# Four PSUM banks for scores, one for up products, and a plan that counts changes of kind on TensorE

## The chip, the cores and the metric

The kernel runs on one core of one Trainium2 chip. The metric is the device time of one execution in microseconds; lower is better. Five engines matter here: TensorE (PE in the profile; PEld is its weight load), VectorE (DVE), ScalarE (ACT), GpSimd (POOL) and SyncE (SP), whose queue issues nearly all DMAs.

## The reference

Attention with a compressive memory over B=4 batches, H=8 heads, S=576 rows and D=64, then two feed-forward layers over the 2304 rows of width 512, with 2048 hidden columns:

```python
scores = causal(scale * q @ k.T)                 # B,H,S,S
local = softmax(scores) @ v
q_p = phi(q)                                     # elu(q) + 1
mem_out = (q_p @ M_prev) / (q_p . z_prev + 1e-6)
a = g * mem_out + (1 - g) * local                # g = sigmoid(beta), one per head
x = a as [2304, 512]
h = x @ w_in;   x = where(h > 0, h, 0.01 * h) @ w_out      # layer 1
h = x @ w_in2;  x = (h - tanh(h)) @ w_out2                 # layer 2
```

## The kernel before

Attention is cut into 32 units (`UNITS`): a kind, a batch and a pair of heads. Kind B has query rows 256 to 575 (tiles 2, 3 and 4 of 128 rows, the last of 64) and runs first, kind A rows 0 to 255 (tiles 0 and 1). A unit loads queries and keys (`qk`) and values (`v` or `va`); multiplies phi(q) by the memory matrix (`mem`, L567); makes the scores (`score`, L647 and L652; two heads side by side on 64 rows of the array each), one group for each of B's three tiles and one for both of A's; VectorE masks them and takes the maximum (`maxi`, L673), ScalarE takes the exponential (L693), the rows are scaled (L727 to L731), TensorE transposes them (`tr_e`, L767 and L779) and multiplies by the values (`pv`, L801), whose PSUM tile begins with the transposed memory part (L745). Four units of one kind and batch make a block of 256 rows; the last 64 rows of every batch make a ninth.

Layer 1 of the first three blocks (`NARROW`) runs beside attention, in eight steps of two weight columns tiles each: an up product of 24 matmuls (L910) into the PSUM tile `up`, ScalarE's leak (L965) out of it, a split into two parts, and 24 down matmuls (L988) into `dn0` and `dn1`, which collect over all eight steps. The weights come as 32 pieces of 512 KB (`w`), which `convert` turns from 64-bit into two 32-bit parts (L838 to L854). The rest of layer 1 and all of layer 2 follow in a fixed loop (L1163 up, L1200 down).

The order of the first part is made when the kernel is built, by `Schedule`: every piece of work has a cost for each engine that could take it, a priority (smallest first) and the tiles that it reads, writes and takes. `run` goes through time and gives each free engine the first piece in order of priority that is ready and whose tiles are free; that order is then each engine's program. `RINGS` says how many buffers a tile has (`s`, `o`, `up`, `dn0` and `dn1` are PSUM banks: 3 + 1 + 2 + 1 + 1 = 8). A unit's priority is its place in `UNITS` plus `OFFSET` of its part; weight pieces have `W1_FROM` (the first 4 x `CUT` the first number, the others the second); TensorE's part of layer 1 comes after attention. `SWITCH` is what TensorE's change from one kind of work (0 layer 1, 1 scores and values, 2 transposes) to another costs. `CALM` holds weight loads back while the DMA queues are that far behind, `AHEAD` bounds how many pieces are in flight, `BIAS` weighs engines against each other. The first `LEND` units put their scores into banks that layer 1 needs later: tiles 2 and 4 into `up`, tile 3 into `dn0` and `dn1`. Units marked in `UNITS` keep their exponentials in tiles of late weights (`LENT`), which can load only after that. `EARLY` weight pieces are loaded at the very start on ScalarE's queue.

Of the kernel before, what the change touches and what calls it, by code (L numbers as in the profile page):

```python
# [9 lines left out]
F32 = mybir.dt.float32  # L10
# [34 lines left out]
SWITCH = {(0, 1): 88.0, (2, 1): 88.0, (0, 2): 45.0}  # L45

CALM = 6000.0
# [50 lines left out]
class Schedule:  # L98
# [60 lines left out]

    def pace(self, t):  # L160
# [24 lines left out]
    def run(self):  # L185
        engines = ("pe", "act", "dve", "pool", "sp")
        free = {"pe": 2500.0, "act": 2200.0, "dve": 3200.0, "pool": 4000.0, "sp": 800.0}
        ready = {e: [] for e in engines}

# [9 lines left out]
        mode = 0  # L199
        port_free = 0.0  # L200
        events = sorted(set(free.values()))
        t = -1.0
        while todo:
# [4 lines left out]
            t = nxt  # L208
            again = True
            while again:  # L210
                again = False
                for e in engines:
                    if free[e] > t:
                        continue
                    for i, (_, _, at, o) in enumerate(ready[e]):
# [56 lines left out]
OFFSET = {"load": 0, "memory": 0.3, "scores": -1, "values": 0.6}  # L272
# [3 lines left out]
LEND = 6  # L276
# [3 lines left out]
UNITS = [(k, b, hp, hp % 2 if k == "A" or b < 1 else 0) for k in "BA" for b in range(4) for hp in range(4)]  # L280
# [3 lines left out]
EARLY = 2  # L284

AHEAD = 5

BIAS = {"act": 1.0, "dve": 1.5, "pool": 1.1}

W1_FROM, W1_STEP = (7.7, 15.7), 0.002  # L290
# [3 lines left out]
CUT = 2  # L294
# [3 lines left out]
def kernel(  # L298
# [40 lines left out]

    early_raw = [wts.tile([128, 1024], I32, name=f"w0_{f}") for f in range(EARLY)]  # L340
# [9 lines left out]
    ginv = const.tile([128, H], F32, name="ginv")  # L350
# [79 lines left out]
    up_p = p1.enter_context(tc.tile_pool(name="up", bufs=2, space=PSUM))  # L430
# [8 lines left out]
    s_p = pa.enter_context(tc.tile_pool(name="s", bufs=3, space=PSUM, side="right"))  # L439
# [33 lines left out]
    class Unit:  # L473
# [14 lines left out]
        def declare(self, pr, prev):  # L488
# [104 lines left out]
            order["p"] = op([("pe", nq * 195)], mem, reads=[ph, mz], alloc=[s, mo], after=in_order("p"))  # L593
# [12 lines left out]
            for tiles in ([[0, 1]] if kind == "A" else [[2], [3], [4]]):  # L606
                if not self.lend:
                    ss = [new("s"), new("s")]
                elif tiles == [3]:
                    ss = [new("dn0"), new("dn1")]  # L610
                else:
                    ss = [new("up"), new("up")]
                c0 = 0
                for t in tiles:
                    nn = min(S, (t + 1) * 128)
                    if kind == "A":
                        et[t - q0] = new(f"e{t if self.alt else t + 2}")
                    else:
                        et[t - q0] = new(f"{'h' if self.alt else 'e'}{t}")
                        if self.alt:  # L620
                            lent.setdefault(LENT[t - 2], []).append(et[t - q0])
                    made[t] = (ss, new("mx"), c0)
                    c0 += nn
                width = c0 if tiles != [4] else S

                def score(e, tiles=tiles, ss=ss):
                    for s in ss:
                        if s.tag == "s":
                            s.tile = s_p.tile([128, 512], F32, name="s")
                        else:  # L630
                            pool = up_p if s.tag == "up" else dn_p
                            s.tile = pool.tile([128, 2, 256], F32, name=s.tag).rearrange("p a b -> p (a b)")
                    for t in tiles:
# [6 lines left out]
                        _, mx, c0 = made[t]  # L640
# [15 lines left out]
                order["s"] = op([("pe", {384: 847, 512: 1060, 576: 1117}[width])], score, reads=[qk], mode=1,  # L656
# [357 lines left out]
    def load_beta(e):  # L1014
        nc.sync.dma_start(out=ginv, in_=beta.partition_broadcast(128))
# [306 lines left out]
```

## Time and profile before

| | us |
|---|---|
| median of 3 runs (lowest, highest) | 1019.71 (1017.88, 1019.96) |
| profiled execution | 1019.15 |
| its span, first to last instruction | 1017.4 |
| TensorE busy | 995.1 |
| VectorE, ScalarE, GpSimd busy | 702.8, 629.6, 196.9 |

The profile is of one execution. Spans and busy times are on the time axis of its first instruction. A line such as L647 is a line of the kernel before. Matmuls are pipelined: their starts are recorded, their ends modelled, so the start of the next one says more than the length. The granted TensorE clock is 0.998 of full speed over the span.

### The profile page before, as it was taken

Reading aid. Unit: us, or ns where it says so; the run is one execution under the profiler, and the core shown is the slowest. Engines: PE = TensorE matmul, PEld = TensorE weight load, DVE = VectorE, ACT = ScalarE, POOL = GpSimd, SP = SyncE. Lnnn points to the kernel's source line nnn. Section 1 sums busy time; section 2 is a strip of 40 time slices with the busy share of each in tenths; the row PEclk is TensorE's granted clock in tenths of the full one; section 3 lists DMA queues with packets and bytes.
Section 4 is the critical chain, followed back from the end, with each engine's and each line's share of the span. In section 5 each row is a group of like instructions: output and inputs, shape, how many; then the busy total and the mean of one; then the engine's idle time right before and its main releaser. Section 6 shows DMA issues by size and latency. Waiting matters only on the chain.

```text
span 1017.4 us, 16055 instructions
## 1 busy us (share of the span) xinstructions
PE 995.1 (98%) x5664; PEld 817.5 (80%) x5664; DVE 702.8 (69%) x1592; ACT 629.6 (62%) x1325; POOL 196.9 (19%) x174
## 2 busy tenths in 40 slices
PE   5899999999999999999999999999999999999998
PEld 3577877778888988888888888888888888888897
DVE  7999999555577366758650225877787787777775
ACT  6987787666598244334423436866676676676664
POOL 1100000000000022222224553222222222222221
PEclk9999999999999999999999999999999999999999
DMA  9564622212252156446534333100100100010010
GB/s 273 188 184 128 192 91 70 69 49 70 59 154 79 63 161 221 144 138 196 184 106 142 117 94 94 43 1 0 63 21 1 63 22 1 1 62 1 1 43 21
DMA packets 92993, 91.77 MB, mean 90 GB/s; under 512 B 45296, under 2 KB 72944, under 8 KB 92912
## 3 DMA queue, kind: packets, MB, share of 16 engines
q1 hardware_dynamic: 91696, 89.44, 28.5%
q10 hardware_dynamic: 1216, 1.31, 0.4%
q8 instruction: 44, 0.72, 0.3%
q14 instruction: 37, 0.30, 0.1%
HBM read 69.75 MB, written 20.97 MB: 89 GB/s over the span
## 4 chain that ended last, share of the span: by engine, by line
PE 91%; DVE 5%; DMA 2%; ACT 1%; issue 1%; SPq 0%; ACTq 0%
PE up L1163 32%; PE dn L1200 32%; PE up L910 6%; PE dn L988 6%; PE o L801 4%; PE s L779 4%; PE s L647 3%; DMA qk<-in_qkt_dram 2%; PE s L567 1%; PE o L745 1%; PE s L652 1%; DVE e L673 1%; DVE cv L849 1%; DVE w L673 1%; DVE e L729 0%
## 5 line engine op out<-in xcount | busy, mean ns | idle before, releaser
L1163 PE MATMUL up<-xs,w 128*128 128x512 f32 (+1 forms) x1536 | 346.1, 375 | 0.0
L1163 PEld LDWEIGHTS up<-xs,w 128*128 128x128 f32 x1536 | 275.8, 188 | 52.9
L468 POOL TENSOR_TENSOR gl<-gf,gh 128x512 fp32r<-128x512 f32 x119 | 154.9, 1301 | 591.7 <-ACT gh L1150 579.5
L1200 PE MATMUL dn<-w,gh 128*128 128x512 f32 x576 | 174.8, 389 | 0.0
L1140 DVE SCALAR_TENSOR_TENSOR gf<-u,w 128x512 f32<-128x512 f32 x72 | 83.8, 1165 | 67.7 <-ACT w L1137 67.6
L1200 PEld LDWEIGHTS dn<-w,gh 128*128 128x128 f32 x576 | 107.6, 188 | 22.0
L1200 PE MATMUL dn<-gh,w 128*128 128x512 f32 x384 | 118.3, 389 | 0.0
L1200 PE MATMUL dn<-w,gl 128*128 128x512 f32 x288 | 109.5, 389 | 0.0
L1117 ACT ACTIVATE gf<-up 128x512 f32<-128x512 f32 x48 | 28.6, 597 | 119.7 <-PE up L1163 116.4
L1131 ACT ACTIVATE u<-up 128x512 f32<-128x512 f32 x72 | 43.0, 598 | 91.8 <-PE up L1163 91.6
L693 ACT ACTIVATE e<-e,mx 128x256 f32<-128x256 f32 (+4 forms) x134 | 76.0, 569 | 21.8 <-DVE mx L673 13.6
L910 PE MATMUL up<-xs,w 128*128 128x256 f32 x576 | 86.8, 290 | 0.0
L1150 ACT ACTIVATE gh<-gf 128x512 fp32r<-128x512 f32 x120 | 74.6, 621 | 16.9 <-DVE gf L1143 16.8
L1200 PEld LDWEIGHTS dn<-gh,w 128*128 128x128 f32 x384 | 72.1, 188 | 15.0
L910 PEld LDWEIGHTS up<-xs,w 128*128 128x128 f32 x576 | 73.6, 189 | 4.7 <-issue 4.7
L1200 PE MATMUL dn<-gl,w 128*128 128x512 f32 x192 | 74.7, 389 | 0.0
L1200 PEld LDWEIGHTS dn<-w,gl 128*128 128x128 f32 x288 | 54.0, 188 | 11.3
L455 ACT ACTIVATE pt<-s 128x320 f32<-128x320 f32 (+4 forms) x132 | 52.7, 440 | 15.9 <-PE s L779 9.3
L673 DVE CUSTOM_DVE_ANT_0 e<-s,mask 128x128 f32<-128x128 f32 (+4 forms) x114 | 46.8, 455 | 22.3 <-PE s L647 19.3
L779 PE MATMUL s<-identr,e 128*128 128x128 f32 x404 | 56.9, 279 | 4.4 <-ACT e L727 1.8
L1143 DVE COPY_PREDICATED gf<-mk,up 128x512 f32<-128x512 int32 x72 | 53.7, 746 | 7.4
L988 PE MATMUL dn<-gh,w 128*128 128x256 f32 x384 | 54.7, 286 | 0.4 <-ACT gh L455 0.4
(130 smaller groups left out, 1506.2 us busy)
## 6 DMA issues: line engine op xcount, KB each, us to landing
w<-in_moe_w_out_dram SPq DMA_DIRECT2D x16, 512.0 KB, 5.5
w<-vs SPq DMA_DIRECT2D x32, 256.0 KB, 2.6
qk<-in_qkt_dram SPq DMA_DIRECT2D x16, 448.0 KB, 3.6
w<-in_moe_w_in_dram SPq DMA_DIRECT2D x14, 512.0 KB, 5.8
v<-in_v_dram SPq DMA_DIRECT2D x16, 320.0 KB, 3.1
x2i<-x2s SPq DMA_DIRECT2D x9, 512.0 KB, 4.1
qk<-in_qkt_dram SPq DMA_DIRECT2D x16, 256.0 KB, 2.8
u<-in_moe_w_in_dram SPq DMA_DIRECT2D x16, 256.0 KB, 2.9
```

The source lines that it names most:

```text
L455: nc.scalar.activation(out=out, in_=in_, func=AF.Copy)
L468: (nc.vector if e == "dve" else nc.gpsimd).tensor_tensor(out=out, in0=in_, in1=high, op=ALU.subtract)
L673: nc.vector.tensor_tensor_reduce(out=out, in0=in0, in1=in1, scale=-scale, scalar=mx.tile[:, 0:1] if t == 4 and j else BIG, op0=ALU.add, op ...
L693: nc.scalar.activation(out=x, in_=x, func=AF.Exp, scale=-1.0, bias=mx.tile[:, k:k + 1], accum_out=sm.tile[:, 2 * i + j:2 * i + j + 1])
L779: nc.tensor.transpose(ss[j].tile[:, a:a + 128], x, ident)
L910: nc.tensor.matmul(ps()[:, s, :], lhsT=w[:, wh * 512 + kt * 128:wh * 512 + (kt + 1) * 128], rhs=xs()[:, xh, kt, :], start=(kt == 0 and j = ...
L988: nc.tensor.matmul(dn[m // 2].tile[:, m % 2, :], lhsT=w[:, wh * 512 + m * 128:wh * 512 + (m + 1) * 128], rhs=gg.tile[:, s * 256:(s + 1) * ...
L1140: nc.vector.scalar_tensor_tensor(out=g, in0=u, scalar=lin, in1=w, op0=ALU.mult, op1=ALU.add)
L1143: nc.vector.copy_predicated(out=g, mask=mk.bitcast(I32), data=h)
L1150: nc.scalar.activation(out=gh, in_=g, func=AF.Copy)
L1163: nc.tensor.matmul(ps[:, s * n:(s + 1) * n], lhsT=w[:, wh * 512 + kt * 128:wh * 512 + (kt + 1) * 128], rhs=xs[:, xh, kt, 0:n], start=(kt = ...
L1200: nc.tensor.matmul(dn, lhsT=lhs, rhs=rhs, start=(fs[0] == 0 and s == 0 and j == 0), stop=(f == NF - 1 and j == 2))
```

## The change

Scores get four PSUM banks instead of three, up products one instead of two. The first units (eight instead of six) borrow only `dn0` and `dn1`, for tile 3; tiles 2 and 4 go to the score banks. `Schedule` knows five kinds of work on TensorE (0 layer 1, 1 scores, 2 transposes, 3 memory products, 4 values) and a cost for every change between two of them, and the costs of the pieces themselves are set anew. Behind a score group it looks for another score group first, behind values for scores or values (`STICK`). Otherwise (`HOLD`) a score group that isn't `paired` comes last: paired means that its banks aren't only score banks, or that all four score banks are free and a second score group is ready or will be. Queries and keys get three buffers; the memory matrix and kind A's values get one each. No weight piece is loaded early; beta's load moves from SP to the start of ScalarE's queue. The order of the units, which of them use lent tiles, the offsets, the due times of the weights, `CALM`, `AHEAD` and `BIAS` get other values.

```diff
-    "qk": 2, "xr": 1, "mz": 2, "v": 1, "va": 2, "ph": 1, "dnm": 2, "mo": 1, "mx": 6, "sm": 3,
-    "e0": 1, "e1": 1, "e2": 1, "e3": 1, "e4": 1, "h2": 1, "h3": 1, "h4": 1, "s": 3, "o": 1, "pt": 4, "x": 2, "xs": 1,
-    "g": 2, "gl": 2, "gh": 2, "up": 2, "dn0": 1, "dn1": 1, "cv": 3,
+    "qk": 3, "xr": 1, "mz": 1, "v": 1, "va": 1, "ph": 1, "dnm": 2, "mo": 1, "mx": 6, "sm": 3,
+    "e0": 1, "e1": 1, "e2": 1, "e3": 1, "e4": 1, "h2": 1, "h3": 1, "h4": 1, "s": 4, "o": 1, "pt": 4, "x": 2, "xs": 1,
+    "g": 2, "gl": 2, "gh": 2, "up": 1, "dn0": 1, "dn1": 1, "cv": 3,
...
-SWITCH = {(0, 1): 88.0, (2, 1): 88.0, (0, 2): 45.0}
-
-CALM = 6000.0
+SWITCH = {
+    (0, 1): 188.0, (0, 2): 2.0, (0, 3): 108.0, (0, 4): 188.0, (1, 0): 209.0, (1, 2): 154.0, (1, 3): 307.0,
+    (1, 4): 200.0, (2, 0): 7.0, (2, 1): 187.0, (2, 3): 109.0, (2, 4): 191.0, (3, 0): 136.0, (3, 1): 324.0,
+    (3, 2): 134.0, (3, 4): 323.0, (4, 0): 206.0, (4, 1): 204.0, (4, 2): 154.0, (4, 3): 309.0,
+}
+
+STICK = {1: (1,), 4: (1, 4)}
+
+HOLD = True
+
+CALM = 20000.0
...
+    def paired(self, o, t):
+
+        if any(h.tag not in ("s", "mx") and h.tag[0] not in "eh" for h in o.alloc):
+            return True
+        free = sum(h is None or not (h.left or h.free_at > t) for h in self.rings["s"])
+        return free >= 4 and (
+            any(x.mode == 1 and x.left == 1 for x in o.users) or any(x[3].mode == 1 and x[3] is not o for x in self.line))
+
...
-                    for i, (_, _, at, o) in enumerate(ready[e]):
+                    line = ready[e]
+                    if e == "pe" and mode in STICK:
+                        line = sorted(line, key=lambda x: x[3].mode not in STICK[mode])
+                    elif e == "pe" and HOLD:
+                        line = sorted(line, key=lambda x: x[3].mode == 1 and not self.paired(x[3], t))
+                    for i, (_, _, at, o) in enumerate(line):
...
-OFFSET = {"load": 0, "memory": 0.3, "scores": -1, "values": 0.6}
+OFFSET = {'load': -0.4, 'memory': -0.1, 'scores': -1.2, 'values': 0.3}
...
-LEND = 6
+LEND = 8
+
+SETS = {"A": (((0, 1),),), "B": (((2,),), ((3,),), ((4,),))}
...
-UNITS = [(k, b, hp, hp % 2 if k == "A" or b < 1 else 0) for k in "BA" for b in range(4) for hp in range(4)]
+UNITS = [
+    ("B", 0, 0, 0), ("B", 0, 1, 1), ("B", 0, 2, 0), ("B", 0, 3, 1), ("B", 1, 0, 0), ("B", 1, 1, 0),
+    ("B", 1, 2, 0), ("B", 1, 3, 1), ("B", 2, 0, 0), ("B", 2, 1, 1), ("B", 2, 2, 0), ("B", 2, 3, 1),
+    ("B", 3, 0, 0), ("B", 3, 1, 0), ("B", 3, 2, 0), ("B", 3, 3, 0), ("A", 0, 0, 0), ("A", 0, 1, 1),
+    ("A", 0, 2, 1), ("A", 0, 3, 0), ("A", 1, 0, 0), ("A", 1, 1, 1), ("A", 1, 3, 1), ("A", 1, 2, 0),
+    ("A", 2, 0, 0), ("A", 2, 1, 1), ("A", 2, 2, 0), ("A", 2, 3, 1), ("A", 3, 0, 0), ("A", 3, 1, 1),
+    ("A", 3, 2, 0), ("A", 3, 3, 1),
+]
...
-EARLY = 2
-
-AHEAD = 5
-
-BIAS = {"act": 1.0, "dve": 1.5, "pool": 1.1}
-
-W1_FROM, W1_STEP = (7.7, 15.7), 0.002
+EARLY = 0
+
+AHEAD = 4
+
+BIAS = {'act': 0.9, 'dve': 1.6, 'pool': 0.8}
+
+W1_FROM, W1_STEP = (9.5, 42.0), 0.05
...
-CUT = 2
+CUT = 7
...
+    ginv = const.tile([128, H], F32, name="ginv")
+    nc.scalar.dma_start(out=ginv, in_=beta.partition_broadcast(128))
...
-    ginv = const.tile([128, H], F32, name="ginv")
...
-    up_p = p1.enter_context(tc.tile_pool(name="up", bufs=2, space=PSUM))
+    up_p = p1.enter_context(tc.tile_pool(name="up", bufs=1, space=PSUM))
...
-    s_p = pa.enter_context(tc.tile_pool(name="s", bufs=3, space=PSUM, side="right"))
+    s_p = pa.enter_context(tc.tile_pool(name="s", bufs=4, space=PSUM, side="right"))
...
-            order["p"] = op([("pe", nq * 195)], mem, reads=[ph, mz], alloc=[s, mo], after=in_order("p"))
+            order["p"] = op([("pe", {2: 206, 3: 429}[nq])], mem, mode=3, reads=[ph, mz], alloc=[s, mo], after=in_order("p"))
...
-            for tiles in ([[0, 1]] if kind == "A" else [[2], [3], [4]]):
-                if not self.lend:
-                    ss = [new("s"), new("s")]
-                elif tiles == [3]:
-                    ss = [new("dn0"), new("dn1")]
-                else:
-                    ss = [new("up"), new("up")]
-                c0 = 0
-                for t in tiles:
-                    nn = min(S, (t + 1) * 128)
-                    if kind == "A":
-                        et[t - q0] = new(f"e{t if self.alt else t + 2}")
-                    else:
-                        et[t - q0] = new(f"{'h' if self.alt else 'e'}{t}")
-                        if self.alt:
-                            lent.setdefault(LENT[t - 2], []).append(et[t - q0])
-                    made[t] = (ss, new("mx"), c0)
-                    c0 += nn
-                width = c0 if tiles != [4] else S
-
-                def score(e, tiles=tiles, ss=ss):
-                    for s in ss:
+            for group in SETS[kind]:
+                banks, cost = [], 0
+                for tiles in group:
+                    tags = ("s", "s")
+                    if self.lend and tiles == (3,):
+                        tags = ("dn0", "dn1")
+                    ss = [new(x) for x in tags]
+                    banks += ss
+                    c0 = 0
+                    for t in tiles:
+                        if kind == "A":
+                            et[t - q0] = new(f"e{t if self.alt else t + 2}")
+                        else:
+                            et[t - q0] = new(f"{'h' if self.alt else 'e'}{t}")
+                            if self.alt:
+                                lent.setdefault(LENT[t - 2], []).append(et[t - q0])
+                        made[t] = (ss, new("mx"), c0)
+                        c0 += min(S, (t + 1) * 128)
+                    cost += {384: 656, 512: 859, 576: 920}[c0]
+
+                def score(e, group=group, banks=banks):
+                    for s in banks:
...
-                            pool = up_p if s.tag == "up" else dn_p
-                            s.tile = pool.tile([128, 2, 256], F32, name=s.tag).rearrange("p a b -> p (a b)")
-                    for t in tiles:
+                            s.tile = dn_p.tile([128, 2, 256], F32, name=s.tag).rearrange("p a b -> p (a b)")
+                    for t in [t for tiles in group for t in tiles]:
...
-                        _, mx, c0 = made[t]
+                        ss, mx, c0 = made[t]
...
-                order["s"] = op([("pe", {384: 847, 512: 1060, 576: 1117}[width])], score, reads=[qk], mode=1,
-                                alloc=ss + [h for t in tiles for h in (et[t - q0], made[t][1])],
-                                after=in_order("s") if tiles[0] == q0 else [order["s"]])
+                own = [h for tiles in group for t in tiles for h in (et[t - q0], made[t][1])]
+                order["s"] = op([("pe", cost)], score, reads=[qk], mode=1, alloc=banks + own,
+                                after=[order["s"]] if "s" in order else in_order("s"))
...
-            op([("pe", nq * 109 - 60)], mem_tr, mode=2, reads=[mo], alloc=[o])
+            op([("pe", nq * 109)], mem_tr, mode=2, reads=[mo], alloc=[o])
...
-                        [("pe", (nq - i0) * 109 * (3 - len(ss)) - 60)], lambda e, j=j, f=tr_e: f(e, j), mode=2,
+                        [("pe", 109 if kt == 4 else (nq - i0) * 109 * (3 - len(ss)))], lambda e, j=j, f=tr_e: f(e, j), mode=2,
...
-            op([("pe", 801 if kind == "A" else 2205)], pv, mode=1, reads=[v_, o] + list({id(x): x for x in pts.values()}.values()),
+            op([("pe", 604 if kind == "A" else 2009)], pv, mode=4, reads=[v_, o] + list({id(x): x for x in pts.values()}.values()),
...
-    def load_beta(e):
-        nc.sync.dma_start(out=ginv, in_=beta.partition_broadcast(128))
-
...
-    sc.op([("sp", 600)], load_beta, writes=[gates], prio=(0, 0.1), dma=[4096])
+    sc.op([("sp", 1)], lambda e: None, writes=[gates], prio=(0, -9), dma=[4096])
```

## Rows read from the trace of the kernel before

**Rows 1.** The page's part on each engine's busy time, share of the span, instructions

```profile
PE 995.1 (98%) x5664; PEld 817.5 (80%) x5664; DVE 702.8 (69%) x1592; ACT 629.6 (62%) x1325; POOL 196.9 (19%) x174
```

**Rows 2.** Busy time by stage: stretch, length, each engine's us and count, clock, DMA

```profile
0.00:25.00 25.00, 13.29 (x60) 7.42 (x61) 19.68 (x73) 16.63 (x38) 4.17 (x15) 0.96 0.95 272
25.00:75.00 50.00, 46.43 (x344) 31.39 (x343) 49.93 (x164) 43.78 (x111) 4.08 (x8) 0.99 0.61 182
75.00:335.00 260.00, 257.33 (x2081) 209.71 (x2080) 196.34 (x688) 191.47 (x515) 7.46 (x16) 1.00 0.33 96
335.00:359.20 24.20, 24.20 (x210) 24.20 (x210) 6.93 (x10) 4.52 (x6) 0.00 (x0) 1.00 0.19 66
359.20:1017.40 658.20, 653.86 (x2978) 544.75 (x2976) 429.89 (x660) 373.25 (x655) 181.17 (x135) 1.00 0.23 75
```

**Rows 3.** The chain that ended last, around 355 us: start, length, what

```profile
353.76 5.60 PE dn L988 x48
```

**Rows 4.** TensorE's timeline, score groups and neighbours: start, length, line, tiles, shape, count

```profile
47.56 0.92 PE L647 MATMUL up<-qk 64*128 64x384 f32 x4
48.31 1.02 PE L647 MATMUL dn<-qk 64*128 64x512 f32 x4
...
102.49 0.95 PE L988 MATMUL dn<-gl,w 128*128 128x256 f32 x6
103.37 1.19 PE L652 MATMUL s<-qk 64*64 64x288 f32 x8
104.49 3.10 PE L910 MATMUL up<-xs,w 128*128 128x256 f32 x24
...
113.47 0.92 PE L647 MATMUL s<-qk 64*128 64x384 f32 x4
114.32 0.63 PE L910 MATMUL up<-xs,w 128*128 128x256 f32 x3
```

**Rows 5.** TensorE's timeline: first score run, first after 75 us, last

```profile
5.12 1.65 PE L647 MATMUL up<-qk 64*128 64x384 f32 x4 [5.12 <-DMA qk<-in_qkt_dram]
...
78.56 0.92 PE L647 MATMUL s<-qk 64*128 64x384 f32 x4
...
324.64 0.93 PE L647 MATMUL s<-qk 64*128 64x128 f32 x8
```

**Rows 6.** Timeline of all engines in the tail, 336.9 to 349 us

```profile
339.60 2.96 PE L910 MATMUL up<-xs,w 128*128 128x256 f32 x24
...
342.40 2.03 PE L988 MATMUL dn<-gh,w 128*128 128x256 f32 x16
342.60 0.60 ACT L965 ACTIVATE g<-up 128x512 f32<-128x512 f32 x1 [1.12 <-PE up L910]
...
345.20 2.96 PE L910 MATMUL up<-xs,w 128*128 128x256 f32 x24
```

**Rows 7.** Loading of the query-key tile: chain's first load, all landings, SP's beta issue

```profile
0.80 4.28 DMA qk<-in_qkt_dram
...
DMA to landing us min/median/max: 2.5/3.1/4.8
...
6.45 1.66 SPq L1015 DMA_DIRECT2D ginv<-in_beta_dram  x1
```

**Rows 8.** TensorE's timeline: first up products; unit 7's middle tile, a lone 512-wide group

```profile
70.34 1.32 PE L910 MATMUL up<-xs,w 128*128 128x256 f32 x9
...
100.22 1.13 PE L647 MATMUL s<-qk 64*128 64x512 f32 x4
```

**Rows 9.** The memory matrix's loads: issue times min/median/max in ns, and landing

```profile
L524 SPq DMA_DIRECT2D mz<-in_M_prev_dram x16: 601/612/742, 2.9 to 293.7; - x16
...
DMA to landing us min/median/max: 2.3/2.6/5.8
```

**Rows 10.** TensorE's timeline: two value runs of kind A, fourteen apart

```profile
270.03 0.87 PE L801 MATMUL o<-pt,va 128*64 128x256 f32 x8
...
333.44 0.87 PE L801 MATMUL o<-pt,va 128*64 128x256 f32 x8
```

More of the change, by code (lines that the diff above doesn't have):

```diff
@@ L188, in run @@
         ready = {e: [] for e in engines}
+        self.line = ready["pe"]
         def enter(o):
@@ L957, in layer1 @@
                 sc.op(
-                    [("pe", 350)], (lambda e, f=three, ff=first_up: ff(e, f)) if one else three,
+                    [("pe", 352)], (lambda e, f=three, ff=first_up: ff(e, f)) if one else three,
                     reads=[xs, w_h[0][2 * p + s]] + ([] if one else [ps]), writes=[ps],
```

## The prediction

> **What bounds the kernel now.** I read first the page's busy times: TensorE works in 98% of the span [rows 1], so only TensorE time counts. Second, busy times by stage [rows 2]. From 359.2 us on, the last 658.2 us are the wide products of layers 1 and 2 with TensorE at 653.86; the change touches none of that work and I move it as a block. What can move is the first stage, which ends when the last down product of the planned part ends, 353.76 + 5.60 = 359.36 us [rows 3]. Its losses are of two sorts. Idle time: 25 - 13.29 = 11.7 us in the first 25 us, 50 - 46.43 = 3.6 us from 25 to 75, 260 - 257.33 = 2.7 us from 75 to 335, none after that. And time in which TensorE counts as busy but changes between kinds of work, which only the timeline shows, third. Score matmuls stand on 64 rows of the array, products and transposes on 128, and around each score group the neighbours run long.
>
> **What one score run costs.** Twenty-four up matmuls in the tail end 2.96 us after their start, the same 24 right behind a score group 3.10 [rows 4, 6]: about 0.14 for the return. Six down matmuls between the memory product and a score group take from 102.49 to 103.37, 0.88 us, against 6 x 2.80/24 = 0.70 at the tail's pace (24 down matmuls from 342.40 to 345.20) [rows 4, 6]: 0.18 for one return and one entry. Inside, a 384-wide group followed by another score group gives the engine on after 0.75 us (47.56 to 48.31), alone after 0.85 (113.47 to 114.32); a 512-wide one behind another takes 1.02, alone 1.13 [rows 4, 8]. So a run taken away saves 0.10 + 0.11 inside and 0.18 at its borders, 0.39 us; where it stood beside the value products, which change the array's shape themselves (128*64), I count only the inside, 0.21. The change's own table says 188 + 209 ns for the way out and back, the same size.
>
> **The change part by part.**
> *Scores in runs.* The timeline has 58 score runs for 64 score groups, the first at 5.12 and the last at 324.64 [rows 5]. Twelve lie before 75 us, 46 behind it (from 78.56 on); 23 of the 46 stand next to a value run. With four banks and the rule that holds a single group back, the 46 could become 22 (one run each for the two units whose middle tile still borrows the down banks, 12 pairs in the eight other units of kind B, 8 pairs of kind A). Twenty-four fewer at the mean of 0.39 and 0.21, 0.30, is 7.2 us; at most 24 x 0.39 = 9.4, at least nothing. A pair needs all four banks free at once, and transposes and memory products draw on the same four, while the plan also lets a lone group follow a value run. I take two thirds: -5.0 us. The twelve early ones lie where TensorE waits anyway: 0, at best 4 x 0.39 = -1.6.
> *Four banks instead of borrowed ones.* Up banks are no longer lent to the first six units. Now up products can't start before the sixth unit's scores; the first is at 70.34 [rows 8]. Afterwards they may start when the first block's input and weights are there, three groups of 2.80 us before the down banks come free behind unit 7's middle tile (100.22 now [rows 8]). That work fits the idle 3.6 us of 25 to 75. I take half, -1.8, ends 0 and -3.6. The later start of down products is covered by the same three groups (8.4 us of work); uncovered it costs up to 2 us: I take +0.3.
> *One up bank.* The next up group must wait until ScalarE has read the last. In the tail that read begins at 342.60 and takes 0.60, while 24 down matmuls hold TensorE until 345.20 [rows 6]: the cover is 2.80 us for a need of 0.64 (339.60 + 2.96 = 342.56 to 343.20) and the signal back, which no row prices; I let it double the need at most. Only the second group of a block has no down product before it: 3 x 0.64 = 1.9 us if attention doesn't fill in; I take +0.5, ends 0 and +3.8.
> The Trainium skill (Perfetto Trace Analysis, Matmuls under Optimizing Tensor Performance) says that independent matmul groups should rotate through different PSUM banks so that one's evacuation overlaps the next group's matmuls. It speaks against this edit; by it each of the 24 groups would pay. The tail's rows go against it here, since other banks' products stand between.
> *The start.* Two early weight loads of 512 KB leave ScalarE's queue, and beta's issue (1.66 us on SP, ahead of the second unit's load) moves to ScalarE's queue. The first query-key load takes 4.28 us against 2.5 to 4.8, median 3.1, of all 32 [rows 7]; its larger form I put at 3.6: -0.7, ends 0 and -1.8. The second load goes out up to 1.66 us sooner; VectorE and ScalarE hold part of that back: -1.0, ends 0 and -1.7. The early weights are not missed: their first use is 70.34, so more than 60 us cover them. The third query-key buffer lets loads run ahead; gain included here.
> *One buffer for the memory matrix and for kind A's values.* The next batch's matrix loads only after the last memory product of this batch: four issues of 0.61 and 2.6 us to landing [rows 9], 5.0 us. Units of kind B follow each other far more slowly; those of kind A come every (333.44 - 270.03)/14 = 4.5 us [rows 10], so three or four handovers can be late by half a microsecond to 5.0. While such a load waits on SP, the loads and stores behind it wait too. MoE work covers: 24.2 us of it are left over even after attention [rows 2]. I take +0.5, ends 0 and +4.
> *Due times, unit order, calm, biases, costs.* 28 weight pieces come due between units 9 and 11 instead of 8 and 24 around units 8 and 16; the last four may only come when the tiles lent up to unit 11 return. VectorE is full either way from 25 to 75 (49.93 of 50 [rows 2]); which of it waits decides. No row prices an order. I bound it by the 2.7 us of idle time from 75 to 335, which may go or double: 0, ends -2.7 and +2.7.
>
> **Sum.** -5.0 - 1.8 + 0.3 + 0.5 - 0.7 - 1.0 + 0.5 = -7.2 us. The profiled execution took 1019.15 us, 1.75 more than its span; 1019.15 - 7.2 = 1011.95, I say 1012.0. It lies 0.56 under the median of the three runs, 1019.71. The ends on the good side add up to -20.8, on the bad side to about +12.5; they won't fall together, and I take 1004 to 1017 as this case's own range.
>
> **The rivals.**
> *Pairs don't form.* The four banks are seldom free together, so that the rule holds groups back and then runs them alone. For it: the ring of score banks carries transposes too. Against it: VectorE, which empties them, is 75% busy from 75 to 335 (196.34 of 260 [rows 2]). Only about four runs go, -1.2 instead of -5.0: 1015.8, with 1013 to 1020 around it.
> *Slower: single buffers in kind A.* Place: the four batches of kind A at the end of attention. If the planner has used up MoE work by then, each handover shows. Price: four handovers of 5.0 us, 20 instead of 0.5, 1031; half covered, 1022. It decides once less than about 5 us of MoE work is left for each batch. Against it: 24.2 us stand behind attention now.
> *Slower: the single up bank.* If up groups run without down products between them, 24 x 0.64 = 15.4 us instead of 0.5: 1027. The tail's order speaks against it; this is the skill's rule as it would act here.
> *More than forecast.* Full pairing and the whole start: below 1002.
>
> **How the numbers follow.** Forecast 0.61, pairs don't form 0.22, single buffers 0.10, up bank 0.04, more than forecast 0.03. About 0.2% (2 us) is what a measurement of this kernel tells from no change. Faster: 0.61 + 0.03 + 0.14 of the 0.22 = 0.78; same: 0.07 of the 0.22; slower: 0.01 + 0.10 + 0.04 = 0.15. The range from 1002 to 1021 leaves out most of the two slower cases and the best one, together under 0.2.
>
> **What would show it.** Right: score runs after 75 us near 30 rather than 46, in the timeline runs with two widths in a row; the first score before 4.5 us; up products before 60 us; the wide products starting near 352 instead of 359.36, with 658 us behind them unchanged. Wrong: up products that wait for ScalarE's read of the up tile, value or memory products that wait for their loads after 250 us, TensorE idle between 75 and 335 well above 2.7 us, or a last stage that is not 658 us.

## The result

The changed kernel takes 1003.79 us, median of four runs (1003.11 to 1004.79), where the kernel before took 1019.84 in the same comparison (1017.88 to 1020.25). The ratio is 0.9847, interval 0.983 to 0.9864. The profiled execution took 1004.79 us; its span is 1003.0.

The page's line on each engine's busy time, after (compare [rows 1]):

```profile
PE 988.3 (99%) x5664; PEld 818.4 (82%) x5664; DVE 687.0 (68%) x1551; ACT 630.2 (63%) x1339; POOL 225.5 (22%) x200
```

TensorE runs the same 5664 matmuls in 6.8 us less. Busy time by stage, after (columns as in [rows 2]; the last two rows cut the span where the wide products begin):

```profile
0.00:25.00 25.00, 16.01 (x80) 9.25 (x80) 17.99 (x72) 15.90 (x39) 6.09 (x18) 0.93 0.71 224
25.00:75.00 50.00, 48.75 (x366) 34.49 (x366) 48.25 (x154) 46.03 (x123) 13.73 (x17) 1.00 0.58 170
75.00:335.00 260.00, 259.77 (x2164) 219.84 (x2161) 184.95 (x663) 192.88 (x520) 24.16 (x30) 1.00 0.37 107
...
0.00:344.90 344.90, 334.43 (x2689) 273.48 (x2690) 255.03 (x891) 258.14 (x685) 43.98 (x65) 1.00 0.42 123
344.90:1003.00 658.10, 653.85 (x2978) 544.91 (x2976) 431.92 (x660) 372.09 (x655) 181.55 (x135) 1.00 0.23 75
```

The same cut of before, at its own first wide product:

```profile
0.00:359.20 359.20, 341.24 (x2689) 272.73 (x2690) 272.89 (x932) 256.39 (x670) 15.71 (x39) 1.00 0.40 118
```

The last stage is the same to 0.1 us: 658.1 against 658.2 in [rows 2]. The whole gain lies in the planned stage, 359.2 - 344.9 = 14.3 us. TensorE's busy time there falls from 341.24 to 334.43, 6.8 us for the same 2689 matmuls; its idle time falls from 18.0 to 10.5, 7.5 us. The idle time goes in three nearly equal parts: 11.7 to 9.0 in the first 25 us, 3.6 to 1.2 from 25 to 75, 2.7 to 0.2 from 75 to 335.

The chain that ended last, after, where the planned part hands over to the wide products (the down group of [rows 3] answers to the first line):

```profile
339.45 5.60 PE dn L1019 x48
345.05 10.93 PE up L1191 x48
```

TensorE's timeline of the start, after (columns as in [rows 4]):

```profile
4.76 1.65 PE L678 MATMUL s<-qk 64*128 64x384 f32 x4 [4.76 <-DMA qk<-in_qkt_dram]
...
10.88 0.92 PE L678 MATMUL s<-qk 64*128 64x384 f32 x4 [1.52 <-DMA qk<-in_qkt_dram]
11.60 1.05 PE L678 MATMUL dn<-qk 64*128 64x512 f32 x4
12.59 1.19 PE L683 MATMUL s<-qk 64*64 64x288 f32 x8
...
17.73 4.39 PE L810 MATMUL s<-identr,e 128*128 128x128 f32 x22
```

and the same stretch of before:

```profile
12.20 0.92 PE L647 MATMUL up<-qk 64*128 64x384 f32 x4 [1.40 <-DMA qk<-in_qkt_dram]
...
16.03 1.66 PE L652 MATMUL up<-qk 64*64 64x288 f32 x8 [2.05 <-DVE mx L673]
...
19.82 0.33 PE L779 MATMUL s<-identr,e 128*128 128x128 f32 x1 [0.42 <-DVE e L729]
```

The first score starts 0.36 us earlier (4.76 against 5.12 in [rows 5]). The larger step is the third group of the second unit: before, it writes a borrowed up bank and waits 2.05 us until VectorE has read it; after, it runs at 12.59 on a score bank, and the long run of transposes starts 2.1 us sooner.

What TensorE waited for in all, after (us in total, times, longest), the three largest:

```profile
PE s L678 <- DMA qk<-in_qkt_dram: 6.3, 2, 4.8
PE o L776 <- DVE mo L618: 2.7, 1, 2.7
PE o L776 <- ACT xr L487: 0.6, 2, 0.3
```

No up product waits for ScalarE's read of the single up bank, no memory product for the single memory matrix, no value product for the single value buffer. The timeline has 34 score runs instead of 58, 23 of them after 75 us instead of 46; 16 instead of 23 of those stand beside a value run. Two groups in one run, and the last run:

```profile
103.01 1.13 PE L678 MATMUL s<-qk 64*128 64x512 f32 x4
104.07 1.19 PE L683 MATMUL s<-qk 64*64 64x288 f32 x8
...
313.49 1.80 PE L678 MATMUL s<-qk 64*128 64x128 f32 x16
```

The last run has all four banks (16 matmuls); in [rows 5] the last one has eight matmuls.

### The profile page after: what moved, and what is told of

It is laid out like the page before. It is cut to its first block, busy times and chain, and to the rows that moved or that the text cites. A ratio compares the mean times of both kernels' runs of the same rounds, so it can differ in the third digit from the quotient of the medians.

```text
span 1003.0 us, 16071 instructions
## 1 busy us (share of the span) xinstructions
PE 988.3 (99%) x5664; PEld 818.4 (82%) x5664; DVE 687.0 (68%) x1551; ACT 630.2 (63%) x1339; POOL 225.5 (22%) x200
## 4 chain that ended last, share of the span: by engine, by line
PE 94%; DVE 2%; ACT 1%; DMA 1%; SPq 0%; issue 0%; POOL 0%; POOLq 0%; DVEq 0%
PE up L1191 33%; PE dn L1228 33%; PE dn L1019 7%; PE up L941 7%; PE s L810 5%; PE o L832 4%; PE s L678 3%; PE s L599 2%; PE s L683 1%; PE o L776 1%; DMA w<-in_moe_w_in_dram 1%; DVE e L704 0%; ACT e L724 0%; DMA w<-in_moe_w_out_dram 0%; PE dn L678 0%
## 5 line engine op out<-in xcount | busy, mean ns | idle before, releaser
L941 PE MATMUL up<-xs,w 128*128 128x256 f32 x576 | 82.1, 287 | 0.0
L724 ACT ACTIVATE e<-e,mx 128x128 f32<-128x128 f32 (+4 forms) x119 | 65.9, 555 | 18.5 <-DVE mx L704 18.0
L487 ACT ACTIVATE pt<-s 128x320 f32<-128x320 f32 (+4 forms) x147 | 56.6, 447 | 9.2 <-PE s L810 7.7
L704 DVE CUSTOM_DVE_ANT_0 e<-s,mask 128x128 f32<-128x128 f32 (+4 forms) x109 | 42.8, 440 | 16.9 <-PE s L678 16.5
L1161 DVE SCALAR_TENSOR_TENSOR hu<-up,u 128x512 f32<-128x512 f32 x72 | 49.4, 687 | 7.0 <-ACT u L1159 3.7
```

What stands on the lines that cost most here:

```text
L487: nc.scalar.activation(out=out, in_=in_, func=AF.Copy)
L724: nc.scalar.activation(out=x, in_=x, func=AF.Exp, scale=-1.0, bias=mx.tile[:, k:k + 1], accum_out=sm.tile[:, 2 * i + j:2 * i + j + 1])
L941: nc.tensor.matmul(ps()[:, s, :], lhsT=w[:, wh * 512 + kt * 128:wh * 512 + (kt + 1) * 128], rhs=xs()[:, xh, kt, :], start=(kt == 0 and j = ...
L1161: nc.vector.scalar_tensor_tensor(out=hu, in0=h, scalar=c4, in1=u, op0=ALU.mult, op1=ALU.mult)
```

## The experiments

The theory at the outset: the gain is the runs that are saved, at about 0.4 us each, plus an earlier start and four banks. Three rivals: a change of kind costs much less, and the busy time falls for another reason; the rules (`STICK`, `HOLD`) do nothing and the banks all of it; or most of it belongs to the one order that the planner happened to find. Differences between kernels of different comparisons are taken from their ratios to the kernel before, times 1019.8 us: after is -15.6 by that.

**The price of a run, first try: p_lone and p_pair.** Added to the changed kernel, in the first layer's wide up products, are 192 groups shaped like scores (64 rows, 384 wide, four matmuls in the profile), one behind every third up matmul, or two behind every sixth.

```diff
-    up2_p = late_pool("up2", 4, space=PSUM)
+    up2_p = late_pool("up2", 2, space=PSUM)
+    price_p = late_pool("price", 1, space=PSUM)
...
+        for j in range(2):
+            d = price_p.tile([128, 512], F32, name=f"price{j}")
+            p = slice(64 * j, 64 * j + 64)
+            nc.tensor.matmul(
+                d[:, 0:384], lhsT=ident[p, :], rhs=w.bitcast(F32)[p, 0:384], start=True, stop=True)
```

> The price of a score run by itself. The changed kernel, and in the wide up products of layer 1's last rounds (48 products of 12 matmuls) a group shaped like a 384-wide score group (two heads on 64 rows each) stands behind every third matmul: 192 lone groups whose result nobody reads; the wide up products have two banks instead of four. To be compared with the kernel that has the same 192 groups in 96 pairs. The run theory, with 0.39 us for each run taken away, expects this kernel's wide layer-1 stretch to be 96 x 0.39 = 37 us longer than that of the paired one. The rival, that the neighbours hide the change of kind, expects under 10 us.

> The same 192 score-shaped groups as in the kernel with lone groups, but two together behind every sixth matmul: 96 runs. The run theory expects it 37 us faster than the lone ones, the rival less than 10 us.

Measured: 1213.11 and 1209.47 us, one execution each, 3.6 apart. TensorE's timeline, p_lone:

```profile
433.04 0.92 PE L1203 MATMUL price<-w,identr 64*128 64x384 f32 x4
433.88 0.96 PE L1192 MATMUL up<-xs,w 128*128 128x512 f32 x3
```

and p_pair:

```profile
432.79 1.92 PE L1203 MATMUL price<-w,identr 64*128 64x384 f32 x8
434.64 1.66 PE L1192 MATMUL up<-xs,w 128*128 128x512 f32 x6
```

One group gives the engine on after 0.84 us, two in a run after 1.85, more than twice as long, where scores in two banks gain ([rows 4]: 0.75 behind each other, 0.85 alone). In the pair the second group wrote the PSUM tile of the first, allocated anew, and between the two of a pair the starts of passes show one step of 0.54 us where a lone group has 0.42. I take that step as a wait that scores in separate banks don't have; no row names it. The comparison says nothing on the price.

**The price, second try: p_lone2 and p_pair2.** The same, 256 wide, with the two groups of a pair in halves of one tile that is allocated once (the edit against the first try).

```diff
+        if group == 0:
+            state["price"] = [price_p.tile([128, 512], F32, name=f"price{g}") for g in range(2)]
+        d = [x[:, 256 * group:256 * group + 256] for x in state["price"]]
...
-            d = price_p.tile([128, 512], F32, name=f"price{j}")
-                d[:, 0:384], lhsT=ident[p, :], rhs=w.bitcast(F32)[p, 0:384], start=True, stop=True)
+                d[j], lhsT=ident[p, :], rhs=w.bitcast(F32)[p, 0:256], start=True, stop=True)
```

> The price of a score run once more. In the earlier pair the second group wrote the banks of the first and waited for them, which the groups of the changed kernel, with four banks, don't. Here the groups are 256 wide and two of them share a tile, written in two halves, so that the second waits for nothing. This one: 192 lone groups in layer 1's last rounds. The run theory, 0.39 us a run, expects this kernel to be 96 x 0.39 = 37 us slower than the one with pairs; from the starts in the earlier lone kernel (entry 0.10, return 0.11, the second pass inside 0.10 and more) 0.3 to 0.4, 29 to 39 us. The rival, hidden changes, expects under 10.

> The same 192 groups of 256 columns in 96 pairs, the second group of a pair in the other half of the tile. Run theory: 29 to 39 us faster than the lone ones; rival: under 10.

Measured: 1172.16 and 1132.25 us, one execution each, with spans of 1170.4 and 1130.5. The difference of 39.9 us over 96 runs is 0.42 us for each run saved (the four runs of the changed kernel lie within 1.7 us, 0.02 for each of 96); the rival with less than 10 us in all falls. It is the price beside wide up products; none was measured beside values. TensorE's timeline, p_lone2:

```profile
433.73 0.70 PE L1205 MATMUL price<-w,identr 64*128 64x256 f32 x4
434.36 0.96 PE L1192 MATMUL up<-xs,w 128*128 128x512 f32 x3
435.25 0.70 PE L1205 MATMUL price<-w,identr 64*128 64x256 f32 x4
```

and p_pair2:

```profile
433.23 1.13 PE L1205 MATMUL price<-w,identr 64*128 64x256 f32 x8
434.30 1.65 PE L1192 MATMUL up<-xs,w 128*128 128x512 f32 x6
435.88 1.14 PE L1205 MATMUL price<-w,identr 64*128 64x256 f32 x8
```

From start to start, a lone group and three up matmuls take 0.63 + 0.89 = 1.52 us, twice that 3.04; the pair and six take 1.07 + 1.58 = 2.65. The 0.39 between them is the same price, read from the timeline.

**The rules taken out: a_nohold and a_stick.** The changed kernel without both rules, and without `HOLD` alone.

```diff
-STICK = {1: (1,), 4: (1, 4)}
+STICK = {}

-HOLD = True
+HOLD = False
```

> The changed kernel without the two rules that keep scores together (no preference behind scores or values, no holding back); banks, costs of changes, due times and start stay. The plan then has 32 score runs after 75 us instead of 23. The run theory: 9 x 0.30 = 2.7 us slower than the changed kernel, about 1006.5. The rival, that the changed kernel is one lucky order among many and that any new plan loses it, expects 5 to 9 us, 1009 to 1013.

> The changed kernel without the rule that holds a lone score group back; the preference for a score group behind scores or values stays. The plan has 29 score runs after 75 us, against 23 with both rules and 32 with neither. Run theory: 6 x 0.42 = 2.5 us for the runs, on top of the 8 to 12 us that a redrawn plan cost in two runs: 1012 to 1018. What is to be told apart is the stretch before 75 us: if the preference for scores gives the early gain, TensorE is idle there for about 10 us as in the changed kernel (9.0 + 1.3); if holding back does, about 12 as without both rules (8.4 + 3.8).

Measured: a_nohold ratio 0.999 (0.998 to 1.0), +14.6 us against the changed kernel; a_stick ratio 1.003 (1.0018 to 1.0043), +18.7. Both lose more than was expected of either, and more than the price of the runs allows: there are 33 and 30 score runs after 75 us instead of 23, ten and seven more, 4.2 and 2.9 us at 0.42. Busy time by stage, a_nohold:

```profile
0.00:25.00 25.00, 16.61 (x72) 9.97 (x72) 17.12 (x69) 15.44 (x38) 6.08 (x18) 0.86 0.72 223
25.00:75.00 50.00, 46.17 (x335) 31.91 (x334) 49.45 (x156) 44.46 (x116) 10.61 (x13) 0.97 0.67 197
...
0.00:359.00 359.00, 343.11 (x2688) 275.95 (x2689) 257.00 (x892) 255.86 (x678) 47.76 (x71) 0.99 0.41 118
```

and a_stick:

```profile
150.00:175.00 25.00, 19.48 (x143) 17.12 (x142) 24.77 (x59) 14.97 (x27) 0.70 (x1) 0.93 0.22 57
...
0.00:358.50 358.50, 341.38 (x2688) 275.99 (x2689) 258.71 (x896) 252.94 (x673) 45.80 (x72) 1.00 0.41 118
358.50:1020.30 661.80, 655.76 (x2978) 544.01 (x2976) 430.25 (x660) 372.41 (x655) 181.81 (x135) 1.00 0.23 75
```

a_nohold's stage is 14.1 us longer. Idle time is 5.4 of it: from 25 to 75 us TensorE idles 3.8 us instead of 1.2, with VectorE full, and after 75 us 3.7 instead of 0.2. Busy time is the larger part, 8.7: the ten runs (4.2), and a granted clock of 0.86 and 0.97 in the first two stretches instead of 0.93 and 1.00 (at most 25 x 0.07 + 50 x 0.03 = 3.3). a_stick's stage is 13.6 us longer. It is as good as the changed kernel to 75 us and loses 5.5 us of TensorE in one place, 150 to 175, with VectorE full; its busy time is 7.0 us longer, of which the runs price 2.9 and the rest is open. Its last stage is 3.7 us longer as well. Part of that is four waits of the wide down products for ScalarE, which the changed kernel doesn't have (us in total, times, longest); the rest is open:

```profile
PE dn L1228 <- ACT ob L487: 1.6, 4, 0.7
```

Two edits of the same rules lose their time in different places. That looks like a new order rather than like a rule, and the next pair tests it.

**The order drawn again: a_353 and a_350.** Only the planner's cost of three up matmuls is changed, by 1 or 2 ns. No engine does anything else by that; but the order comes out anew.

```diff
-                    [("pe", 352)], (lambda e, f=three, ff=first_up: ff(e, f)) if one else three,
+                    [("pe", 350)], (lambda e, f=three, ff=first_up: ff(e, f)) if one else three,
```

(a_353: 353 in the same place.)

> The changed kernel with one number of the plan moved by 1 ns: the cost of three up matmuls 353 instead of 352. Nothing of what the change does is undone, 23 or 24 score runs after 75 us, but the plan is drawn again. The run theory expects the changed kernel's time within 2 us, 1002 to 1006. The rival of the lucky order expects 1008 to 1013, as the plan's own finish is 8 us later.

> A second neutral redraw of the changed kernel's plan: the cost of three up matmuls 350 ns instead of 352 (the value of the kernel before), all else as changed; 23 score runs after 75 us. With 353 the time was 1013.3. If that was an outlier and the changed parts alone decide, 1003 to 1006; if the changed kernel is the lucky draw, 1009 to 1015.

Measured: a_353 ratio 0.9935 (0.9917 to 0.9953), +9.0 us against the changed kernel; no profile of it is read. a_350 1015.94 us, ratio 0.9961 (0.9947 to 0.9975), +11.6. Both side with the lucky order. One order by itself takes much the same time again: in p_lone, p_pair, p_lone2 and p_pair2, which keep the changed kernel's plan, the wide products start at 343.2 to 343.6 us, in the changed kernel at 344.9. Busy time by stage, a_350 (two rows cut where the granted clock changes):

```profile
0.00:356.60 356.60, 338.92 (x2689) 274.84 (x2689) 262.82 (x900) 255.08 (x674) 43.69 (x67) 0.99 0.40 119
...
150.00:175.00 25.00, 20.62 (x143) 17.71 (x142) 24.85 (x59) 14.88 (x26) 0.00 (x0) 0.86 0.24 76
...
160.00:166.50 6.50, 3.02 (x21) 2.42 (x20) 6.50 (x16) 4.04 (x7) 0.00 (x0) 1.00 0.01 3
166.50:173.30 6.80, 5.89 (x25) 4.39 (x26) 6.65 (x17) 3.53 (x6) 0.00 (x0) 0.50 0.33 87
```

and the changed kernel in the same stretch:

```profile
150.00:175.00 25.00, 24.98 (x206) 21.99 (x205) 25.00 (x70) 20.78 (x46) 2.67 (x3) 1.00 0.41 135
```

a_350 has the same 23 score runs after 75 us, and its first 75 us are as good (16.89 and 48.31 us busy). Its idle time from 75 to 335 is 260 - 252.12 = 7.9 us instead of 0.2, most of it here. From 166.5 to 173.3 the granted clock is 0.50, the lower of the two levels (1.2 and 2.4 GHz), with TensorE busy for 5.89 us: up to half of that, 2.9 us, is lost. With 7.7 us of idle time that is 10.6 of the stage's 11.7. TensorE's timeline in the gap, a_350:

```profile
161.55 0.50 PE L941 MATMUL up<-xs,w 128*128 128x256 f32 x2 [0.68 <-ACT w L487]
162.47 1.44 PE L941 MATMUL up<-xs,w 128*128 128x256 f32 x10 [0.43 <-DVE w L500]
166.28 0.66 PE L1019 MATMUL dn<-gh,w 128*128 128x256 f32 x2 [2.37 <-ACT w L487]
```

Up and down products of layer 1 both wait for weights that ScalarE and VectorE are still taking apart. In the changed kernel attention stands between them, and TensorE idles 0.02 of the 25 us, though VectorE is just as full there.

**What fails in that gap: a_350_nolow.** The order of a_350, but VectorE's instruction for the low part of the planned weight pieces is left out (it stays in the plan's costs), so that the lowest bits of these weights are zero in the products.

```diff
-                f(raw.tile[:, :], g.tile[:, :])
+                if f is not c_low:
+                    f(raw.tile[:, :], g.tile[:, :])
```

> The redrawn plan with 350 ns (1015.9 us), in its own order, but without VectorE's last step of the conversion of the 32 planned weight pieces (the one that puts in the low word; the lowest bits of these weights stay zero). The plan still counts the step, so every engine's order is the same; only VectorE has 0.69 us less for each piece. In that redraw TensorE stood idle for 7.9 us behind 75 us, most between 100 and 200, while VectorE was 24.5 to 24.9 us busy in each 25. If a redraw loses because VectorE's conversions are late there, the idle time goes and the time is 1003 to 1008. If it loses by something in TensorE's own order, it stays at 1013 to 1016.

Measured: 1010.85 us, ratio 0.9918 (0.9898 to 0.9937): 4.4 of the 11.6 us come back, so neither expectation holds alone. Busy time by stage, a_350_nolow:

```profile
150.00:175.00 25.00, 21.76 (x155) 18.79 (x155) 22.04 (x54) 16.82 (x32) 2.63 (x2) 0.86 0.23 62
...
156.00:162.50 6.50, 3.88 (x28) 3.26 (x27) 5.99 (x17) 4.90 (x9) 0.00 (x0) 1.00 0.01 3
162.50:169.30 6.80, 6.17 (x27) 4.37 (x27) 6.37 (x16) 3.68 (x8) 0.00 (x0) 0.50 0.39 94
```

and the longest wait in the gap, on TensorE's timeline:

```profile
162.19 0.60 PE L1020 MATMUL dn<-gh,w 128*128 128x256 f32 x2 [1.87 <-ACT w L487]
```

VectorE now has 3 us to spare from 150 to 175, and the idle time of TensorE from 75 to 335 falls from 7.9 to 3.4 us. Nearly all that is left is the gap, 3.2 us from 150 to 175 where a_350 has 4.4, and ScalarE's step ends its longest wait as before. So VectorE's step is less than half of the loss. The rest I read from the traces as the order itself, layer 1's steps standing together ahead of the last weights instead of between attention's; no run separates that.

**The parts on the kernel before: b_psum8, b_psum8_hold, b_start.** First the banks alone: four for scores, one for up products, lending only `dn0` and `dn1`, for tile 3, to eight units, with before's rules and costs.

```diff
-"s": 3, ... "up": 2,
+"s": 4, ... "up": 1,
...
-LEND = 6
+LEND = 8
...
-                if not self.lend:
+                if not self.lend or tiles != [3]:
                     ss = [new("s"), new("s")]
-                elif tiles == [3]:
-                    ss = [new("dn0"), new("dn1")]
                 else:
-                    ss = [new("up"), new("up")]
+                    ss = [new("dn0"), new("dn1")]
```

> One part alone, on the kernel before: four score banks, one up bank, eight units that borrow only the down banks. The old costs of changes and pieces stay and no rule keeps scores together; even so the plan has 34 score runs after 75 us instead of 46, as many as with the rules on top. If the banks alone bring runs and the early gain, 1012 to 1015, as with the rules (1013.5); if the rules and the costs are needed, 1017 to 1021.

Then the same with the change's table of costs, kinds, `STICK` and `HOLD`.

```diff
-SWITCH = {(0, 1): 88.0, (2, 1): 88.0, (0, 2): 45.0}
+SWITCH = {
+    (0, 1): 188.0, (0, 2): 2.0, (0, 3): 108.0, (0, 4): 188.0, (1, 0): 209.0, (1, 2): 154.0, (1, 3): 307.0,
...
+STICK = {1: (1,), 4: (1, 4)}
+
+HOLD = True
```

> One part alone, on the kernel before: four score banks and one up bank, eight units that borrow the down banks, five kinds with the new costs of changes and pieces, and the two rules that keep scores together. Start, single buffers, due times, unit order, offsets and biases stay as before. The plan has 34 score runs after 75 us instead of 46. Run theory: 12 x 0.30 = 3.6 us and up to 1.8 us of early up products, 1014 to 1016. The theory that the rest, tuned to the order, carries the gain expects no change or a loss, 1018 to 1024. If the better costs alone do it, about 1009.

And the start alone: no early weights, beta's load on ScalarE's queue.

```diff
-EARLY = 2
+EARLY = 0
...
+    nc.scalar.dma_start(out=ginv, in_=beta.partition_broadcast(128))
```

> One part alone, on the kernel before: no early weight pieces and beta's load at the head of ScalarE's queue. The prediction gave this 1.7 us: 1018 if the plan's redraw costs nothing. Against it: the kernel with the new banks and the old start had its first score at 4.79 us, as early as with the new start (4.76). If the start's edits count for nothing, the first score comes between 4.5 and 5.1, the second unit's third group still waits for an up bank, and TensorE's idle time in the first 25 us stays near 11 us; the time then is 1020 give or take a redraw, 1012 to 1028.

Measured: b_psum8 ratio 0.9923 (0.9905 to 0.994), -7.9 us; b_psum8_hold 0.9936 (0.9921 to 0.995), -6.5; b_start 1.0001 (0.9989 to 1.0013), 0. Busy time in b_psum8, from 25 to 75 us and in the planned stage, and its third group of the second unit:

```profile
25.00:75.00 50.00, 47.04 (x355) 32.12 (x352) 48.68 (x162) 42.80 (x113) 1.82 (x5) 1.00 0.55 157
0.00:352.30 352.30, 338.83 (x2688) 273.54 (x2689) 267.31 (x931) 250.21 (x669) 18.85 (x41) 0.99 0.42 120
...
16.00 1.86 PE L650 MATMUL s<-qk 64*64 64x288 f32 x6 [1.58 <-DVE mx L671]
```

The planned stage of b_psum8_hold:

```profile
0.00:351.70 351.70, 336.36 (x2689) 272.89 (x2690) 270.52 (x940) 248.41 (x662) 17.26 (x40) 1.00 0.41 121
```

The same rows of b_start, with the first 25 us and its first scores:

```profile
0.00:25.00 25.00, 16.48 (x73) 10.33 (x75) 18.06 (x72) 15.41 (x38) 2.89 (x14) 0.86 0.84 258
25.00:75.00 50.00, 48.36 (x368) 33.75 (x365) 48.56 (x162) 44.27 (x115) 2.43 (x6) 1.00 0.58 170
0.00:358.40 358.40, 344.16 (x2689) 274.70 (x2690) 272.88 (x935) 255.20 (x672) 11.76 (x35) 0.99 0.41 118
...
4.57 1.65 PE L648 MATMUL up<-qk 64*128 64x384 f32 x4 [4.57 <-DMA qk<-in_qkt_dram]
```

The plan drawn with the banks alone brings half of the gain: busy time -2.4 us (36 score runs after 75 us instead of 46), idle time -4.5. With the rules and costs on top TensorE is busy another 2.5 us less and idle 1.9 more; the intervals of the two overlap, so nothing measurable is added. Nor do pairs form there: 35 score runs after 75 us instead of 36. b_start has its first score at 4.57 and 3.7 us less idle time in the stage, but 2.9 us more busy time; the total doesn't move. Its idle time in the first 25 us is 8.5 us, not near 11 as expected if the start's edits count for nothing. Of the busy time up to 2 us is the clock: 0.86 instead of 0.96 in the first 25 us, 1.00 instead of 0.99 in the next 50 (25 x 0.10 - 50 x 0.01).

## Why the prediction was right, and where it was not

The sign and the place were right: 14.3 us in the planned stage, none in the last. The size was not: the sum has 7.2 us, half of that. The measured time lies 8.2 us below the forecast, 0.2 below the case's own range (1004 to 1017) and inside the wider one (1002 to 1021). Busy time gave 6.8 us where the sum has 5.0, idle time 7.5 where the other terms come to 2.2. That the gain is twice the forecast is in part the luck of the draw: the two redraws, -6.6 and -4.0 us, differ from the changed kernel by one cost of 1 or 2 ns and lie nearer to the forecast. Each step by its own number:

- *Price of a run.* Predicted 0.39 us away from value runs, measured 0.42 out and back. The Trainium skill (TensorEngine Tiling (Array Packing), Key Properties) says that a change of tiling mode drains TensorE; the 0.42 us agrees with that, though no trace shows the drain itself.
- *Scores in runs, -5.0.* The runs after 75 us fell to 23, not to about 30: I took two thirds of the 24 that the four banks allow, and nearly all came, which takes the whole plan: 33 are left without the rules (a_nohold), 35 with banks, rules and costs on before's other numbers (b_psum8_hold). By the forecast's own prices, 16 runs away from values at 0.39 and 7 beside them at 0.21 make 7.7 us. Busy time fell by 6.8. The rival that pairs don't form is refuted for the changed kernel. The term was too small by about 2 us.
- *Four banks instead of borrowed ones, -1.8.* The first up product is at 59.43 instead of 70.34 [rows 8], and the idle time from 25 to 75 us falls by 2.3. The first down product comes at 91.72 instead of 84.97 without any wait. The number came out, but that the banks bring it isn't shown: the idle time from 25 to 75 us is 3.0 with the banks alone (b_psum8) and 3.8 with the banks in a_nohold, and it is 1.6 in b_start, which still borrows the up banks, where before has 3.6.
- *The start, -0.7 and -1.0.* Idle time in the first 25 us falls by 2.7, so the size was fair, but by luck. The sign named for it, a first score before 4.5 us, didn't come. First scores at 4.57 (b_start) and 4.76 (after) stand beside 4.67 and 4.79 in b_psum8 and b_psum8_hold, which have the old loads: the early weights and beta's issue don't set it, and b_start, which changes these alone, gains nothing in all. Its idle time in the first 25 us does fall by 3.2, but b_psum8, with the old loads, is idle for 8.4 us there too. What moved in the changed kernel is the third group of the second unit, which no longer waits for a borrowed up bank. Banks alone don't do that (16.00 in b_psum8); banks with the new rules and costs do (13.59 in b_psum8_hold), and so does the changed kernel without the rules (12.32 in a_nohold).
- *One up bank, +0.5 (0 to 3.8).* No wait in the changed kernel; b_psum8 has one of 1.2 us on ScalarE's read, b_psum8_hold one of 0.7. The Trainium skill's rule that matmul groups should rotate through PSUM banks (Perfetto Trace Analysis, Optimizing Tensor Performance) is kept by the down products that stand between, as the tail in [rows 6] suggested. That rival is refuted.
- *Single buffers, +0.5 (0 to 4).* No such wait in the changed kernel. a_nohold and a_stick wait 2.2 and 1.4 us for the memory matrix's loads, all between 276 and 295 us, so the term is real in other orders, but far from the rival's 20 us.
- *Due times, unit order and the rest, 0 (-2.7 to +2.7).* This is the step that failed. Its bound came from the idle time that before had from 75 to 335 us. That idle time did vanish, 2.4 of the 2.7 us. But what an order can lose isn't bounded by what one order lost: one nanosecond in a planner's cost moved the time by 9.0 us, two by 11.6, with the number of score runs unchanged in the second. Ends of some 10 us would have fitted these two redraws.

The account as the runs give it: the banks on before's other numbers bring about 8 us, half of the gain; the rules and costs on top, and the start, bring nothing that can be measured there. Each of these is one plan, drawn once, and a redraw moved the changed kernel by more than 8 us, so these shares aren't shown to hold in another order. The other half belongs to the whole plan of the changed kernel. The rules have a share in it, but how much can't be told: taking them out costs 14.6 to 18.7 us, and a neutral redraw by itself costs 9.0 to 11.6. How far the kernel before was itself a good or a poor draw wasn't tried, nor the edits to due times and unit order one by one.

## What to carry to other kernels

Where one engine is busy nearly all of the time, look for time that counts as busy: count the changes of kind on it, price one from two neighbouring rows, and ask what keeps equal work apart; here PSUM banks lent to another stage were a part of it (46 runs fell to 36 with the banks alone). Judge a greedy planner's edit over several neutral redraws (a cost moved by a nanosecond), not over one order; a single comparison mixes the edit with luck, here of 9 to 12 us. When pricing an operation with added work, make sure that the added work doesn't wait on itself: pairs that wrote one PSUM tile twice, allocated anew, showed 3.6 us, pairs in halves of a tile 39.9.

## What the hardware showed that was not expected

Gaps of a few microseconds in TensorE's work cost more than themselves here. In a_350 TensorE was busy 3.02 of the 6.5 us from 160 to 166.5, its longest single wait 2.37 us; from 166.5 to 173.3 the granted clock was 0.50, although TensorE was busy again for 5.89 of these 6.8 us. In a_350_nolow, which has the same gap 4 us earlier, it was 0.50 from 162.5 to 169.3 with TensorE busy for 6.17 us, behind 3.88 busy of 6.5 and a longest wait of 1.87. The changed kernel has no such gap there, and a clock of 1.00.
